# Moving the last z2 tile behind v, splitting k's first shifted copies, z2's bias on GpSimd, and a new order of products and gates

## The chip, the cores and the metric

The kernel runs on one core of a Trainium2 chip. The metric is the device time of one execution in microseconds (us). Of the kernel before, three runs are shown: 201.68, 201.68 and 201.16, median 201.68. The profile is of an execution of its own.

The engines are TensorE (PE, with PEld for its weight loads), VectorE (DVE), ScalarE (ACT), GpSimd (POOL) and SyncE (SP), which here only issues transfers. Each works through its own list of instructions in order; semaphores join them. Transfers issued by SP, ScalarE and GpSimd go through DMA queues.

## The reference

The input x (2048 positions by 512) is normalised over its 512 channels to xn. Two branches are computed from xn, and x is added:

```python
def _A_ref(x, wqkv, wo):            # 32 heads of 16 channels, W = 8 positions, dilation 2
    q, k, v = heads of (x @ wqkv)
    idx = pos[:, None] - 2 * arange(8)[None, :]     # this position and 7 before it
    logits = einsum('bhsd,bhswd->bhsw', q, k[idx]) * 16 ** -0.5   # masked where idx < 0
    o = einsum('bhsw,bhswd->bhsd', softmax(logits), v[idx])
    return o @ wo

def _B_ref(x, w_in, w_sp, b_sp, w_out):             # Fh = 688
    z = gelu(x @ w_in)
    z1, z2 = z[..., :Fh], layernorm(z[..., Fh:])
    g = einsum('ts,bsf->btf', w_sp, z2) + b_sp[None, :, None]
    return (z1 * g) @ w_out

out = x + _A_ref(xn, wqkv, wo) + _B_ref(xn, w_in, w_sp, b_sp, w_out)
```

## The kernel before

The 2048 positions are 16 tiles of 128. All steps are named, each has a list of steps that it needs (`op_(name, needs, f)`), and the order on every engine is written out by hand in five lists at the end (`pe`, `act`, `dve`, `pool`, `sp`). The lists set the order on each engine; waits between engines follow from the data.

TensorE's list is one long row: transposes of xn (T), the z2 half of x @ w_in (z0 to z15, L231), k and q in turns (k0 ... q7, L324), v (v0 to v7, L324), the z1 half (y2 to y15, L231; y0 and y1 earlier), the mixing by w_sp (M0 to M15, L467: each tile M_j sums over all 16 tiles of z2), then the two output products (gf, re: L511 and L516; ao: L523). z, k, q, v, y and M write into three PSUM tiles `mm` in turn, so each waits until the tile of the product three places before it has been read: by `h` (gelu of z), `kc`, `qc`, `vc` (copies of k, q, v), `yg` (gelu of y) or `G` (M plus b_sp), all on ScalarE.

z2 is normalised per position. For tiles 8 to 15 ScalarE takes the sum in the gelu (h, L249) and the sum of squares (sq, L277). Then for four tiles at a time, 8 to 11 and 12 to 15: `zs` on VectorE (L281 to L283) makes mean and variance, `zr` on GpSimd (L287, a scale, and L288, a power) the reciprocal root, `zb` (L292) the bias, and `zn` on ScalarE (L304) scales each tile in place. M0 needs all `zn`.

The attention has four channels of a head at a time (c = 0 to 3) and two halves of the positions (th = 0, 1). k's rows carry 16 positions from the half before them; these shifted copies are `kh` (L342 and L343, two DMAs each). kh0 and kh1 are issued by SP, kh2 and kh3 by GpSimd, and `vh` is the same for v, on SP. For each c and th VectorE forms the products `m` (L358, two instructions of 2.29 us), `f` folds their second half onto the first by an adding DMA issued by GpSimd (L366, two DMAs; f00 alone is an add on VectorE), and `p` (L371, or L373 and L374) sums into the logits. There are four buffers for the products: a product takes a buffer when the `p` of its last user is done. Then follow the softmax (X, e, u, i, C) and the weighted sum of v, twelve VectorE instructions a half (a0.0 to a1.11, L425 to L438), between which stand the gates `g` (L483: z1 times G). Each gated tile is turned by SP (`U`, L473 to L476) and is needed by the output products: the tiles 8 to 15 by gf2.

Of W_sp, 256 rows at a time are loaded and transposed by SP (W0 to W7) into three buffers. The third is also a product buffer, so W2 waits until all `p` are done (HW).

Of the kernel before, what the change touches and what calls it, by code (L numbers as in the profile page):

```python
# [10 lines left out]
ALU = mybir.AluOpType  # L11
# [5 lines left out]
NT = S // P  # L17
# [9 lines left out]
FH = 688  # L27
# [15 lines left out]
def kernel(  # L43
# [13 lines left out]
    V = nc.vector  # L57
    A = nc.scalar
    G = nc.gpsimd
    PE = nc.tensor  # L60
    SP = nc.sync

    x2 = A_x.rearrange("b s d -> (b s) d")
# [13 lines left out]
    zsum = sb.tile([P, NT], F32, name="zsum")  # L77
    zsq = sb.tile([P, NT], F32, name="zsq")
    zmean = sb.tile([P, NT], F32, name="zmean")
    zvar = sb.tile([P, NT], F32, name="zvar")  # L80
    zrstd = sb.tile([P, NT], F32, name="zrstd")
    zbias = sb.tile([P, NT], F32, name="zbias")
    b16 = sb.tile([NT, P], BF16, name="b16")
# [15 lines left out]
    k_c = [r[:, QC:QC + KC].rearrange("p (d t s) -> p d t s", d=DC, t=2) for r in qk_c]  # L99
# [50 lines left out]
    def op_(name, after, f):  # L150
        assert name not in do, name
        do[name], needs[name] = f, list(after)
# [125 lines left out]

    def z2_stats(i, n):
        s = slice(i, i + n)  # L280
        V.tensor_scalar(zmean[:, s], zsum[:, s], 1.0 / FH, None, ALU.mult)  # L281
        V.tensor_tensor(zvar[:, s], zmean[:, s], zmean[:, s], ALU.mult)  # L282
        V.scalar_tensor_tensor(zvar[:, s], zsq[:, s], 1.0 / FH, zvar[:, s], ALU.mult, ALU.subtract)  # L283

# [4 lines left out]

    def z2_bias(i, n):  # L290
        s = slice(i, i + n)
        V.scalar_tensor_tensor(zbias[:, s], zmean[:, s], -1.0, zrstd[:, s], ALU.mult, ALU.mult)  # L292

    for i in range(0, 8, 4):
        op_(f"zr{i}", [f"zt{i + x}" for x in range(4)], lambda i=i: z2_bn_root(i, 4))
    for i in range(8, NT, 4):
        op_(f"zs{i}", [f"sq{i + x}" for x in range(4)], lambda i=i: z2_stats(i, 4))
        op_(f"zr{i}", [f"zs{i}"], lambda i=i: z2_root(i, 4))
        if i in ZACT:
            op_(f"zb{i}", [f"zr{i}"], lambda i=i: z2_bias(i, 4))  # L300
# [39 lines left out]
    def halo(eng, x):  # L340
        y = x.rearrange("p d t s -> p (d t) s")
        eng.dma_start(y[H:P, :, 0:HALO], y[0:P - H, :, GS:GS + HALO])  # L342
        eng.dma_start(x[0:H, :, 1, 0:HALO], x[P - H:P, :, 0, GS:GS + HALO])  # L343

    for c in range(NC):
        op_(f"kh{c}", [f"kc{2 * c}", f"kc{2 * c + 1}"], lambda c=c: halo(SP if c < 2 else G, k_c[c]))
    op_("vh", [f"vc{p}" for p in range(8)], lambda: halo(SP, vp[:]))


    last = {}  # L350

    def products(c, th):
        for a in range(2):
            pr = ph[BUF[c, th]][a].rearrange("p (w b s) -> p w b s", w=W, b=2)
            k = k_c[c][:, 2 * a:2 * a + 2, th, :]
            k = bass.AP(k.tensor, k.offset + HALO - DIL * (W - 1), [k.ap[0], [DIL, W], k.ap[1], [1, GS]])
            q = q_c[c][:, 2 * a:2 * a + 2, th, :].unsqueeze(1).broadcast_to([P, W, 2, GS])
            V.tensor_tensor(pr, q, k, ALU.mult)  # L358

    def fold(c, th):  # L360
        x = PU // 4
        if (c, th) == (0, 0):
            V.tensor_tensor(ph[0][0], ph[0][0], ph[0][1], ALU.add)
            return
        for n in range(2):
            G.dma_start(*[h[:, n * x:(n + 1) * x] for h in ph[BUF[c, th]]], accum_op=ALU.add)  # L366

    def logits(c, th):
        pr = ph[BUF[c, th]][0].rearrange("p (w b s) -> p w b s", w=W, b=2)
        if c == 0:  # L370
            V.tensor_tensor(a_sb[:, th], pr[:, :, 0], pr[:, :, 1], ALU.add)  # L371
        else:
            V.tensor_tensor(pr[:, :, 0], pr[:, :, 0], pr[:, :, 1], ALU.add)  # L373
            V.tensor_tensor(a_sb[:, th], a_sb[:, th], pr[:, :, 0], ALU.add)  # L374

    for c, th in BUF:
        n = f"{c}{th}"
        b = BUF[c, th]
        over = {2: ALLN + ALLX, 3: [f"p{1}{0}"] + [f"{a}{p}" for a in "qk" for p in range(8)]}.get(b, [])
        op_(f"m{n}", over + [f"qc{2 * c}", f"qc{2 * c + 1}", f"kh{c}"] + ([last[b]] if b in last else []),  # L380
            lambda c=c, th=th: products(c, th))
        op_(f"f{n}", [f"m{n}"], lambda c=c, th=th: fold(c, th))
        op_(f"p{n}", [f"f{n}"], lambda c=c, th=th: logits(c, th))
        last[b] = f"p{n}"
# [174 lines left out]
    for n, c in enumerate(halves):  # L559
        i = groups[3][3]  # L560
# [2 lines left out]


    pe = """wu T0a T0 z0a z0A T1 z0B T2 z1 T3 z2 T4 z3 T5 z4 T6 z5 T7 B z6 z7 y0 y1 z8 z9 z10 z11 z12 z13 z14
        k0 k1 q0 q1 z15 k2 k3 q2 q3 k4 k5 q4 q5 k6 k7 q6 q7
        v0 v1 v2 v3 v4 v5 v6 v7 y2 y3 y4 y5 y6 y7 y8 y9 y10 y11 y12 y13 y14 y15
        M0 M1 M2 M3 M4 M5 M6 M7 M8 M9 M10 M11 M12 M13 M14 M15
        gf0 gf1 re0 re1 ao0 ao1 gf2 re2 re3 ao2 ao3""".split() + [f"gf3.{i}" for i in tail[:3]] + ["gfl0", "gfl1"]
    for n in pe:  # L570
        a, x = n[0], n[1:]
# [19 lines left out]
    op_("EL", ["yg15"], lambda: A.preload_act_table_set("natural_log_exp_and_others"))  # L591

    act = """wz0 wz1 GL Tc0a Tc0 Tc1 Tc2 h0 Tc3 h1 Tc4 h2 Tc5 h3 Tc6 h4 Tc7 Bc h5 h6 h7 yg0 yg1 h8 h9 sq8 h10 h11 sq9 h12 h13 h14 sq10
        kc0 sq11 kc1 qc0 sq12 qc1 h15 kc2 sq13 kc3 sq14 qc2 sq15 qc3 kc4 kc5 qc4 qc5 kc6 kc7 qc6 qc7
        vc0 zn8 vc1 zn9 vc2 zn10 vc3 zn11 vc4 zn12 vc5 zn13 vc6 zn14 vc7 zn15
        yg2 yg3 yg4 yg5 yg6 yg7 yg8 yg9 yg10 yg11 yg12 yg13 yg14 yg15 EL
        G0 e0 G1 i0 e1 G2 i1 G3 G4 G5 G6 G7 G8 G9 G10 G11 G12 G13 G14 G15""".split()
    act += [f"E{i}" for n in (0, 1) for i in groups[n]]
    dve = """b0 ag0 b1 ag1 n0a n0 b2 ag2 n1 b3 ag3 n2 b4 ag4 n3 b5 ag5 n4 b6 ag6 b7 n5""".split()
    for i in range(6, NT):  # L600
        dve += [f"ag{i + 1}"] * (i + 1 < NT) + [f"b{i + 2}"] * (i + 2 < NT) + [f"n{i}"]
    dve += """zt0 zt1 zt2 zt3 zt4 zt5 zn0 zn1 zn2 zn3 zt6 zt7 zn4 zn5 zn6 zn7
        m00 f00 p00 m01 zs8 m10 zb8 zs12 m11 p01 zb12 m20 p10 m21 p11 m30 p20 m31 p21 p30 X0 p31 HW u0 X1 C0 g0 a0.0 u1 a0.1 C1 g1 g2
        a0.2 g3 a0.3 g4 a0.4 g5 a0.5 a0.6 g6 a0.7 g7 a0.8 a0.9 g8 a0.10 a0.11 g9 g10 a1.0 a1.1 g11 a1.2 g12 a1.3 g13
        a1.4 g14 a1.5 a1.6 g15 a1.7 a1.8 a1.9 a1.10 a1.11""".split()
    OUT = [i for n in range(3) for i in groups[n]] + tail[:3]
    dve += [f"F{i}" for i in OUT] + ["Fl0", "Fl1"]
    pool = ["b16"] + [f"gr{i}" for i in range(NT)] + "zr0 zr4 f01 zr8 kh2 f10 zr12 kh3 f11 f20 f21 f30 f31".split()
    sp = """x0 x1 x2 x3 x4 x5 x6 x8 wy x12 wk wq wv t8 t9 t10 t11 t12 t13 t14 t15 W0 kh0 W1 kh1 vh
        W2 W3 LO0 LO1 W4 U0 W5 LO2 LO3 U1 U2 W6 LO4 U3 U4 W7 U5 U6 U7 U8 U9 U10 R0 U11 U12 U13 R1 U14 U15""".split()  # L610
    sp += [f"S{i}" for i in OUT] + ["Sl0"]
    act.append("Sl1")
# [52 lines left out]
```

## Time and profile before

| | |
|---|---|
| runs shown, median | 201.68 us (201.16 to 201.68) |
| the profiled execution's own time | 201.17 us |
| its span in the profile | 199.4 us |
| TensorE busy | 194.3 us, 97% |
| VectorE busy | 177.5 us, 89% |
| ScalarE busy | 89.7 us, 45% |
| GpSimd busy | 39.0 us, 20% |
| granted TensorE clock | 1.00 in every stage looked at |

The span is what the engines' records cover; the execution's own time is 1.8 us longer. Times in the rows that follow are from the start of the span. A row of the chain in order of time is: start, length, what. A row of a timeline is: start, length, engine, line, operation, output <- input, shapes, count, and in brackets the idle time of that engine ahead of it with what ended it. Consecutive instructions of one kind are merged into one row; an instruction's record can begin a little ahead of the end of the one before. "SPq" rows are issues of transfers. A row "DMA to landing" gives the shortest, median and longest time from the start of an issue to the arrival of its data.

### The profile page before, as it was taken

Reading aid. Unit: us, or ns where it says so; the run is one execution under the profiler, and the core shown is the slowest. Engines: PE = TensorE matmul, PEld = TensorE weight load, DVE = VectorE, ACT = ScalarE, POOL = GpSimd, SP = SyncE. Lnnn points to the kernel's source line nnn. Section 1 sums busy time; section 2 is a strip of 40 time slices with the busy share of each in tenths; the row PEclk is TensorE's granted clock in tenths of the full one; section 3 lists DMA queues with packets and bytes.
Section 4 is the critical chain, followed back from the end, with each engine's and each line's share of the span. In section 5 each row is a group of like instructions: output and inputs, shape, how many; then the busy total and the mean of one; then the engine's idle time right before and its main releaser. Section 6 shows DMA issues by size and latency. Waiting matters only on the chain.

```text
span 199.4 us, 4530 instructions
## 1 busy us (share of the span) xinstructions
PE 194.3 (97%) x1935; PEld 122.5 (61%) x1935; DVE 177.5 (89%) x204; ACT 89.7 (45%) x130; POOL 39.0 (20%) x67
## 2 busy tenths in 40 slices
PE   7899999999999999999999999999999999999993
PEld 2576666666777766666666666666666654443441
DVE  4999895899898999988999999999999999997234
ACT  2597797795559996672542311112221110043000
POOL 5677122002999330330000000000000000000000
PEclk9999999999999999999999999999999999999999
DMA  5999476840977999998099999999996679914233
GB/s 163 349 361 230 89 123 139 144 81 0 196 132 140 197 196 147 185 167 168 11 234 229 188 168 227 237 123 258 198 230 60 118 219 233 154 19 133 81 105 105
DMA packets 68964, 32.58 MB, mean 163 GB/s; under 512 B 56912, under 2 KB 67024, under 8 KB 68816
## 3 DMA queue, kind: packets, MB, share of 16 engines
q1 hardware_dynamic: 65568, 24.12, 59.5%
q0 software_dynamic: 2176, 7.40, 20.0%
q10 hardware_dynamic: 1200, 0.77, 1.4%
q8 instruction: 15, 0.25, 0.5%
q14 instruction: 5, 0.04, 0.1%
HBM read 10.03 MB, written 2.10 MB: 61 GB/s over the span
## 4 chain that ended last, share of the span: by engine, by line
PE 95%; DMA 3%; DVE 1%; ACTq 0%; DVEq 0%; issue 0%
PE mm L467 37%; PE mm L324 21%; PE mm L231 19%; PE mm L523 7%; PE mm L511 7%; DMA wts<-in_B_w_in_dram 3%; PE aux L511 2%; PE mm L516 1%; PE aux L213 1%; ACTq L239 0%; DVE z L561 0%; DVEq L660 0%; DVE wsp L129 0%; PE aux L523 0%; DVE qk L139 0%
## 5 line engine op out<-in xcount | busy, mean ns | idle before, releaser
L467 PE MATMUL mm<-z,wsp 128*128 128x344 bf16 x512 | 74.8, 309 | 0.0
L467 PEld LDWEIGHTS <-wsp 128*128 128x128 bf16 x512 | 50.1, 98 | 24.6
L324 PE MATMUL mm<-xnT,wts 128*32 128x512 bf16 x768 | 41.9, 380 | 0.0
L231 PE MATMUL mm<-wts,xnT 128*128 128x344 bf16 x256 | 39.0, 309 | 0.5 <-ACT xnT L216 0.5
L324 PEld LDWEIGHTS <-wts 128*32 128x32 bf16 x768 | 29.5, 140 | 12.0 <-issue 0.6
L425 DVE TENSOR_TENSOR prod<-vp,a_sb 128x4096 bf16<-128x4096 bf16 x16 | 36.1, 2285 | 0.0
L481 ACT ACTIVATE qk<-mm,b_col 128x688 bf16<-128x688 f32 x16 | 13.3, 830 | 45.3 <-PE mm L467 38.3
L231 PEld LDWEIGHTS <-xnT 128*128 128x128 bf16 x256 | 24.4, 98 | 13.0 <-issue 1.0
L358 DVE TENSOR_TENSOR prod<-qk 128x4096 bf16<-128x4096 bf16 x12 | 27.0, 2288 | 1.8 <-DMA qk<-qk 1.6
L429 DVE TENSOR_TENSOR prod<-prod,prod 128x8192 bf16<-128x8192 bf16 x6 | 26.5, 4420 | 0.0
L337 ACT CAST qk<-mm 128x1024 bf16<-128x1024 f32 x16 | 16.2, 1012 | 7.8 <-PE mm L324 7.8
L313 ACT ACTIVATE z<-mm 128x688 bf16<-128x688 f32 x16 | 11.8, 748 | 5.7 <-PE mm L231 5.3
L366 POOL DMA_DIRECT2D prod<-prod x10 | 8.7, 1022 | 28.3 <-DVE zvar L282 16.0
L523 PE MATMUL mm<-wts,xnT 32*128 32x512 bf16 x192 | 14.2, 374 | 0.0
L511 PEld LDWEIGHTS <-qk 128*128 128x128 bf16 x85 | 8.2, 98 | 9.4 <-issue 0.8
L511 PE MATMUL mm<-wts,qk 128*128 128x512 bf16 x60 | 13.6, 379 | 0.0
L249 ACT ACTIVATE z<-mm 128x688 bf16<-128x688 f32 x16 | 11.9, 745 | 1.9 <-PE mm L231 1.8
L170 DVE BATCH_NORM_STATS2 stats<-z 128x6 f32<-128x512 bf16 x16 | 10.8, 673 | 1.7 <-DMA z<-in_A_x_dram 1.7
L523 PEld LDWEIGHTS <-xnT 32*128 32x128 bf16 x256 | 6.3, 93 | 7.7 <-issue 0.8
L556 DVE TENSOR_TENSOR z<-mm,wsp 128x512 bf16<-128x512 f32 x6 | 3.8, 684 | 8.0 <-PE mm L523 4.8
L550 ACT CAST z<-mm 128x512 bf16<-128x512 f32 x6 | 3.2, 598 | 13.7 <-PE mm L523 12.3
L177 POOL TENSOR_TENSOR rstd<-rstd,mhalf 128x1 f32<-128x1 f32 x16 | 9.0, 561 | 1.3
(82 smaller groups left out, 169.6 us busy)
## 6 DMA issues: line engine op xcount, KB each, us to landing
prod<-prod POOLq DMA_DIRECT2D x10, 512.0 KB, 7.6
wts<-in_A_wo_dram SPq DMA_DIRECT2D x4, 512.0 KB, 6.3
wsp<-in_A_x_dram SPq DMA_DIRECT2D x2, 1024.0 KB, 6.5
out_dram<-z SPq DMA_DIRECT2D x15, 128.0 KB, 1.8
wts<-in_A_wqkv_dram SPq DMA_DIRECT2D x3, 512.0 KB, 8.6
z<-in_A_x_dram SPq DMA_DIRECT2D x2, 512.0 KB, 6.4
wsp<-z POOLq DMA_DIRECT2D x2, 512.0 KB, 6.5
wsp<-wts POOLq DMA_DIRECT2D x2, 512.0 KB, 8.9
```

Of the source, the lines that this page charges most:

```text
L231: PE.matmul(t[:, hh, 0:FHALF], xnT[:, kc, i * P:(i + 1) * P], w_z[part][:, kc, hh * FHALF:(hh + 1) * FHALF], start=(kc == 0), stop=(kc == ...
L249: A.activation(z2[:, i, :].rearrange("p (a b) -> p a b", a=2), t[:, :, 0:FHALF], ACT.Gelu_apprx_tanh, **total)
L313: op_(f"yg{i}", [f"y{i}"], lambda: A.activation(z1u[:, i, 0:FH].rearrange("p (a b) -> p a b", a=2), t[:, :, 0:FHALF], ACT.Gelu_apprx_tanh))
L324: PE.matmul(t[32 * g:32 * g + 32, dd, :], w, r, start=(kc == 0), stop=(kc == C - 1), tile_position=(0, 32 * g))
L337: op_(f"{a}c{p}", [f"{a}{p}"], lambda: A.copy(home(a, p), t[:].rearrange("p d (t s) -> p d t s", t=2)))
L358: V.tensor_tensor(pr, q, k, ALU.mult)
L425: return lambda: V.tensor_tensor(dst, vp[:, :, th, off:off + GS], a_sb[:, th, W - 1 - w].unsqueeze(1).broadcast_to([P, DH, GS]), ALU.mult)
L429: return lambda: V.tensor_tensor(dst, dst, x, ALU.add)
L467: PE.matmul(t[:, hh, 0:FHALF], w[:, k, (j % 2) * P:(j % 2 + 1) * P], z2[:, k, hh * FHALF:(hh + 1) * FHALF], start=(k == 0), stop=(k == NT ...
L481: lambda: A.activation(gs[j % 3].rearrange("p (a b) -> p a b", a=2), t[:, :, 0:FHALF], ACT.Identity, bias=b_col[:, j:j + 1]))
L511: PE.matmul(po[i][:, c], uT[th][:, m, t0:t0 + P], wout[:, m, c], start=(start and m == 0), stop=(stop and m == MF - 1))
L523: PE.matmul(po[groups[n][g]], op[32 * g:32 * g + 32, th, d, s * P:(s + 1) * P], wo_r[32 * g:32 * g + 32, d, :], start=(start and d == 0), ...
```

## The change

Four things are edited; the arithmetic stays.

- In TensorE's list z15 goes from between q1 and k2 to between v7 and y2. In ScalarE's list h15 and sq15 go behind vc7. zn8 to zn11 start one copy of v later, and zn12 to zn15 stand between yg9 and yg13, each ahead of a gelu of z1.
- kh0 becomes two steps, kh0a behind kc0 and kh0b behind kc1, each with two DMAs for two of the four channels. The first half of m00 depends on the first pair alone.
- zs8 and zs12 write the mean with the other sign, and the bias is a plain product on GpSimd in place of one on VectorE. zb8 stands behind zr8 and ahead of kh2 in GpSimd's list.
- In VectorE's list zs12 goes from behind m10 to behind m30, in GpSimd's list zr12 goes from behind f10 to behind f30 with zb12 after it, ahead of f31. The gates g13, g14 and g15 stand later among the steps of a1.

```diff
-        V.tensor_scalar(zmean[:, s], zsum[:, s], 1.0 / FH, None, ALU.mult)
+        V.tensor_scalar(zmean[:, s], zsum[:, s], -1.0 / FH, None, ALU.mult)
...
-        V.scalar_tensor_tensor(zbias[:, s], zmean[:, s], -1.0, zrstd[:, s], ALU.mult, ALU.mult)
+        G.tensor_tensor(zbias[:, s], zmean[:, s], zrstd[:, s], ALU.mult)
...
-        op_(f"kh{c}", [f"kc{2 * c}", f"kc{2 * c + 1}"], lambda c=c: halo(SP if c < 2 else G, k_c[c]))
+        if c == 0:
+            for a in range(2):
+                op_(f"kh0{'ab'[a]}", [f"kc{a}"], lambda a=a: halo(SP, k_c[0][:, 2 * a:2 * a + 2]))
+        else:
+            op_(f"kh{c}", [f"kc{2 * c}", f"kc{2 * c + 1}"], lambda c=c: halo(SP if c < 2 else G, k_c[c]))
...
# pe
-        k0 k1 q0 q1 z15 k2 k3 q2 q3 k4 k5 q4 q5 k6 k7 q6 q7
-        v0 v1 v2 v3 v4 v5 v6 v7 y2 y3 y4 y5 y6 y7 y8 y9 y10 y11 y12 y13 y14 y15
+        k0 k1 q0 q1 k2 k3 q2 q3 k4 k5 q4 q5 k6 k7 q6 q7
+        v0 v1 v2 v3 v4 v5 v6 v7 z15 y2 y3 y4 y5 y6 y7 y8 y9 y10 y11 y12 y13 y14 y15
# act
-        kc0 sq11 kc1 qc0 sq12 qc1 h15 kc2 sq13 kc3 sq14 qc2 sq15 qc3 kc4 kc5 qc4 qc5 kc6 kc7 qc6 qc7
-        vc0 zn8 vc1 zn9 vc2 zn10 vc3 zn11 vc4 zn12 vc5 zn13 vc6 zn14 vc7 zn15
-        yg2 yg3 yg4 yg5 yg6 yg7 yg8 yg9 yg10 yg11 yg12 yg13 yg14 yg15 EL
+        kc0 sq11 kc1 qc0 sq12 qc1 kc2 sq13 kc3 sq14 qc2 qc3 kc4 kc5 qc4 qc5 kc6 kc7 qc6 qc7
+        vc0 vc1 zn8 vc2 zn9 vc3 zn10 vc4 zn11 vc5 vc6 vc7 h15 sq15
+        yg2 yg3 yg4 yg5 yg6 yg7 yg8 yg9 zn12 yg10 zn13 yg11 zn14 yg12 zn15 yg13 yg14 yg15 EL
# dve
-        m00 f00 p00 m01 zs8 m10 zb8 zs12 m11 p01 zb12 m20 p10 m21 p11 m30 p20 m31 p21 p30 X0 p31 HW u0 X1 C0 g0 a0.0 ...
-        ... a1.3 g13 a1.4 g14 a1.5 a1.6 g15 a1.7 a1.8 a1.9 a1.10 a1.11
+        m00 f00 p00 m01 zs8 m10 m11 p01 m20 p10 m21 p11 m30 zs12 p20 m31 p21 p30 X0 p31 HW u0 X1 C0 g0 a0.0 ...
+        ... a1.3 a1.4 g13 a1.5 g14 a1.6 a1.7 g15 a1.8 a1.9 a1.10 a1.11
# pool
-    zr0 zr4 f01 zr8 kh2 f10 zr12 kh3 f11 f20 f21 f30 f31
+    zr0 zr4 f01 zr8 zb8 kh2 f10 kh3 f11 f20 f21 f30 zr12 zb12 f31
# sp
-    ... t15 W0 kh0 W1 kh1 vh
+    ... t15 W0 kh0a kh0b W1 kh1 vh
```

More of the change, by code (lines that the diff above doesn't have):

```diff
@@ L379 @@
         over = {2: ALLN + ALLX, 3: [f"p{1}{0}"] + [f"{a}{p}" for a in "qk" for p in range(8)]}.get(b, [])
-        op_(f"m{n}", over + [f"qc{2 * c}", f"qc{2 * c + 1}", f"kh{c}"] + ([last[b]] if b in last else []),
+        op_(f"m{n}", over + [f"qc{2 * c}", f"qc{2 * c + 1}"] + (["kh0a", "kh0b"] if c == 0 else [f"kh{c}"]) + ([last[b]] if b in last else []),
             lambda c=c, th=th: products(c, th))
@@ L602 @@
     dve += """zt0 zt1 zt2 zt3 zt4 zt5 zn0 zn1 zn2 zn3 zt6 zt7 zn4 zn5 zn6 zn7
-        m00 f00 p00 m01 zs8 m10 zb8 zs12 m11 p01 zb12 m20 p10 m21 p11 m30 p20 m31 p21 p30 X0 p31 HW u0 X1 C0 g0 a0.0 u1 a0.1 C1 g1 g2
-        a0.2 g3 a0.3 g4 a0.4 g5 a0.5 a0.6 g6 a0.7 g7 a0.8 a0.9 g8 a0.10 a0.11 g9 g10 a1.0 a1.1 g11 a1.2 g12 a1.3 g13
-        a1.4 g14 a1.5 a1.6 g15 a1.7 a1.8 a1.9 a1.10 a1.11""".split()
+        m00 f00 p00 m01 zs8 m10 m11 p01 m20 p10 m21 p11 m30 zs12 p20 m31 p21 p30 X0 p31 HW u0 X1 C0 g0 a0.0 u1 a0.1 C1 g1 g2
+        a0.2 g3 a0.3 g4 a0.4 g5 a0.5 a0.6 g6 a0.7 g7 a0.8 a0.9 g8 a0.10 a0.11 g9 g10 a1.0 a1.1 g11 a1.2 g12 a1.3
+        a1.4 g13 a1.5 g14 a1.6 a1.7 g15 a1.8 a1.9 a1.10 a1.11""".split()
     OUT = [i for n in range(3) for i in groups[n]] + tail[:3]
     dve += [f"F{i}" for i in OUT] + ["Fl0", "Fl1"]
-    pool = ["b16"] + [f"gr{i}" for i in range(NT)] + "zr0 zr4 f01 zr8 kh2 f10 zr12 kh3 f11 f20 f21 f30 f31".split()
-    sp = """x0 x1 x2 x3 x4 x5 x6 x8 wy x12 wk wq wv t8 t9 t10 t11 t12 t13 t14 t15 W0 kh0 W1 kh1 vh
+    pool = ["b16"] + [f"gr{i}" for i in range(NT)] + "zr0 zr4 f01 zr8 zb8 kh2 f10 kh3 f11 f20 f21 f30 zr12 zb12 f31".split()
+    sp = """x0 x1 x2 x3 x4 x5 x6 x8 wy x12 wk wq wv t8 t9 t10 t11 t12 t13 t14 t15 W0 kh0a kh0b W1 kh1 vh
         W2 W3 LO0 LO1 W4 U0 W5 LO2 LO3 U1 U2 W6 LO4 U3 U4 W7 U5 U6 U7 U8 U9 U10 R0 U11 U12 U13 R1 U14 U15""".split()
```

## The prediction

> **What bounds the kernel now.** I read the chain that ended last first, then TensorE's neighbours on each engine around its stages. The page gives the chain by engine, and the chain in order of time gives the stages (start us, length us, what):
>
> ```profile
> PE 95%; DMA 3%; DVE 1%; ACTq 0%; DVEq 0%; issue 0%
> ```
> ```profile
> 28.38 7.07 PE mm L324 x128
> 35.45 1.27 PE mm L231 x8
> 36.72 34.70 PE mm L324 x534
> 71.43 16.44 PE mm L231 x112
> 87.87 74.67 PE mm L467 x512
> ...
> 179.15 4.42 PE mm L511 x20
> ```
>
> TensorE has no gap from the first product to the last: k and q around z15 (28.38 to 71.43, v included), y2 to y15 (71.43 to 87.87, 16.44/14 = 1.174 us each), then M0. The other engines matter only where they make TensorE late. There is nothing to take from TensorE's own work except a change of product form around z15, while every microsecond by which M0 begins after 87.87 is a microsecond on the end. So the question is what releases y13, y14, y15 and M0 afterwards. Each takes the PSUM tile that the gelu three products earlier (yg10 to yg13) empties on ScalarE, and the change puts zn12 to zn15 in ScalarE's order right there.
>
> ScalarE before (the copies and gelus by time; the bracket is the idle time in front):
>
> ```profile
> 30.32 1.01 ACT L337 CAST qk<-mm 128x1024 bf16<-128x1024 f32 x1 [0.31 <-PE mm L324]
> 33.78 1.01 ACT L337 CAST qk<-mm 128x1024 bf16<-128x1024 f32 x1 [0.71 <-PE mm L324]
> ...
> 60.31 0.97 ACT L304 ACTIVATE z<-z,zbias,zrstd 128x688 bf16<-128x688 bf16 x1
> 61.18 1.00 ACT L337 CAST vp<-mm 128x1024 bf16<-128x1024 f32 x1
> ...
> 73.48 1.41 ACT L313 ACTIVATE z<-mm 128x688 bf16<-128x688 f32 x2
> 80.90 0.74 ACT L313 ACTIVATE z<-mm 128x688 bf16<-128x688 f32 x1 [0.42 <-PE mm L231]
> ```
>
> The last row is yg9, done at 81.64. A zn takes 0.87 start to start (60.31 to 61.18), a gelu 0.67 back to back (1.41 - 0.74).
>
> VectorE and GpSimd before:
>
> ```profile
> 35.85 4.50 DVE L358 TENSOR_TENSOR prod<-qk 128x4096 bf16<-128x4096 bf16 x2 [1.65 <-DMA qk<-qk]
> 43.85 4.48 DVE L358 TENSOR_TENSOR prod<-qk 128x4096 bf16<-128x4096 bf16 x2
> 48.26 0.16 DVE L281 TENSOR_SCALAR zmean<-zsum 128x4 f32<-128x4 f32 x1
> 50.97 2.29 DVE L358 TENSOR_TENSOR z<-qk 128x4096 bf16<-128x4096 bf16 x1
> 54.17 0.16 DVE L292 SCALAR_TENSOR_TENSOR zbias<-zmean,zrstd 128x4 f32<-128x4 f32 x1 [0.92 <-POOL zrstd L288]
> 54.73 4.49 DVE L358 TENSOR_TENSOR prod<-qk 128x4096 bf16<-128x4096 bf16 x2
> 59.13 1.22 DVE L371 TENSOR_TENSOR a_sb<-prod 128x2048 bf16<-128x2048 bf16 x1
> 61.28 0.16 DVE L292 SCALAR_TENSOR_TENSOR zbias<-zmean,zrstd 128x4 f32<-128x4 f32 x1 [0.92 <-POOL zrstd L288]
> 65.87 1.22 DVE L373 TENSOR_TENSOR wsp<-wsp 128x2048 bf16<-128x2048 bf16 x1
> 75.36 4.50 DVE L358 TENSOR_TENSOR prod<-qk 128x4096 bf16<-128x4096 bf16 x2
> 79.77 1.22 DVE L373 TENSOR_TENSOR prod<-prod 128x2048 bf16<-128x2048 bf16 x1
> 82.28 4.50 DVE L358 TENSOR_TENSOR prod<-qk 128x4096 bf16<-128x4096 bf16 x2
> ```
> ```profile
> 48.65 1.81 POOL L366 DMA_DIRECT2D prod<-prod  x2 [16.05 <-DVE zvar L282]
> 50.54 0.57 POOL L287 TENSOR_SCALAR zvar<-zvar 128x4 f32<-128x4 f32 x1
> 51.19 2.95 POOL L288 TENSOR_TENSOR zrstd<-zvar,mhalf 128x4 f32<-128x4 f32 x1
> 54.11 0.88 POOL L342 DMA_DIRECT2D qk<-qk  x1
> 55.58 1.85 POOL L366 DMA_DIRECT2D wsp<-z  x2
> 57.50 1.77 POOL L287 TENSOR_SCALAR zvar<-zvar 128x4 f32<-128x4 f32 x1
> 59.35 1.89 POOL L288 TENSOR_TENSOR zrstd<-zvar,mhalf 128x4 f32<-128x4 f32 x1
> 80.15 1.70 POOL L366 DMA_DIRECT2D prod<-prod  x2 [5.28 <-DVE prod L358]
> ```
>
> A tiny GpSimd operation ends when a VectorE product of two inputs does. The scale at 57.50 ends at 59.27, just behind m11 (54.73 + 4.49 = 59.22). The power at 59.35 ends at 61.24, which is 0.89 behind the end of p01's add (60.35); the one at 51.19 ends at 54.14, 0.88 behind m10 (53.26). So each costs the rest of the VectorE instruction that is running, plus 0.05 (scale) or 0.89 (power).
>
> **Part by part.**
>
> *k's first copies in two pieces.* One pair of DMAs becomes two: kh0a behind kc0 (done 31.33), kh0b behind kc1. On the SP queue and to landing:
>
> ```profile
> 33.09 0.76 SPq L342 DMA_DIRECT2D qk<-qk  x1
> 33.90 0.64 SPq L343 DMA_DIRECT2D qk<-qk  x1
> ```
> ```profile
> DMA to landing us min/median/max: 1.8/1.8/1.8
> ```
>
> kh0a's two issues (0.76 + 0.64) end by 32.8, ahead of kh0b's place at 33.09, so W1, kh1 and vh behind them on SP are not moved. Its second copy is issued at about 32.2 and lands at 34.0. m00's first half then waits only for qc0 (33.78 + 1.01 = 34.79); kh0b lands near 35.7, and the second half starts at 37.1. VectorE is 1.0 us earlier: m00 34.85, m01 ends 47.35. Were the issue not hidden, its 1.4 us would fall on VectorE, which has cover.
>
> *z15 behind v.* k2 to v7 move 1.27 us forward and z15 takes 70.16 to 71.43; y2 stays. The switch to z15 and back disappears: 7.07 us for 32 groups of four is 0.221 a group, 34.70 for 160 is 0.217, so about 0.1 us is gained (bounds 0 and 0.2). h15 and sq15 follow vc7 and end near 73.3, so yg2 stays near 73.4: nothing. But zs12 now can't be earlier than 73.3.
>
> *Bias on GpSimd.* Two VectorE instructions of 0.16 go, and their waits of 0.92 each. zs12 leaves its place behind m10 too. By the rows, m11 starts 54.73 - 53.26 = 1.47 sooner behind m10, and m20, which now directly follows p01, some 1.1 sooner. A tiny TENSOR_TENSOR on GpSimd, zb8, is added: its nearest row is the scale, the rest of a VectorE instruction plus 0.05. It stands ahead of kh2 and f10 in GpSimd's queue. With everything 0.97 earlier: f01 47.68 to 49.49, scale to 50.13, power to 53.17, then zb8 waits for m11's first half (52.2 + 2.29) and ends at 54.55. kh2's two issues take 55.58 - 54.11 = 1.47 and f10 is issued at 56.1, against 55.58 before. f10's landing, before (two halves):
>
> ```profile
> DMA to landing us min/median/max: 4.7/6.5/8.4
> ```
>
> The second half starts 0.95 into the 1.85 and lands 8.4 later: 64.9 before, 65.45 now. kh2 must have landed when m20 starts; for m20 (4.49) to hide in front of 65.45 it has until 60.9, five microseconds after issue. So p10 begins at 65.45, against 65.87: **VectorE's gain goes into a new wait for f10.** p10, m21, p11, m30 last from 65.87 to 79.86 = 13.99, so m30 ends at T = 79.44.
>
> *zs12 behind m30, zr12 and zb12 behind f30.* zs12: three instructions, 0.5 us (48.26 to m10 at 48.76 before). Then VectorE has p20's two adds (to T + 2.9; 79.77 to 82.28 is 2.51) and m31's halves (to T + 5.2 and T + 7.4). GpSimd: f30 starts T + 0.29 (80.15 - 79.86) and takes 1.70, T + 2.0. The scale waits for p20: T + 2.96. The power starts in m31's first half, T + 5.2, + 0.89 = T + 6.1. zb12 waits for m31's second half: T + 7.5. That is **87.0**. Bounds: 5.3 where one boundary is caught instead of missed, 8.5 where the power holds VectorE up (below). I take 7.5, by the rows of zr8 and zr12, which each missed theirs. f31 is queued behind zb12 on GpSimd and needs m31, which ends at T + 7.4 itself: it goes out 0.1 us later than it could, and with it p31, the release of W2's buffer and W2, which M4 needs some 19 us behind M0's start: nothing.
>
> *zn12 to zn15 among the gelus.* ScalarE stands behind yg9 (81.64) until 87.05. Then zn12, yg10, zn13, yg11, zn14, yg12, zn15, yg13: 4 x 0.87 + 3 x 0.67 + 0.74 = 6.2 us, as y10 to y12 are long done. yg10 is done at 88.7, so y13, due at 84.35, begins 4.4 late; y14 and y15 wait for yg11 and yg12 (about 0.4 each), M0 for yg13: 93.3. **M0 is 5.4 us late**, and nothing behind it can give that back.
>
> *Gates g13 to g15 later.* g15 comes behind one more sum:
>
> ```profile
> 164.47 0.51 DVE L483 TENSOR_TENSOR z<-qk,z 128x688 bf16<-128x688 bf16 x1
> 164.90 4.42 DVE L429 TENSOR_TENSOR prod<-prod,prod 128x8192 bf16<-128x8192 bf16 x1
> ...
> 170.81 1.23 SPq L476 DMA_TRANSPOSE qk<-z  x1
> ```
>
> By about 4.6 us, to 169.6; its transposes would be issued 1 us later than before, to 173, and are needed at 179.15 (later still with M late). Cost nothing; without that cover it is at most that 1 us.
>
> Sum: 201.17 (the profiled execution; span 199.4) + 5.4 - 0.1 = **206.5**. The median of the runs shown, 201.68, stands 0.5 above the profiled one.
>
> The Trainium skill, SBUF — State Buffer, section "Who interferes with whom", says that a VectorE instruction with two SBUF inputs and a GpSimd instruction that reads SBUF exclude each other, whichever came first holding the port pair for its whole length. The waits above agree (57.50 to 59.27); in both power rows VectorE was waiting anyway, so no row shows the other direction.
>
> **The rivals.**
>
> *The power holds VectorE back.* If VectorE can't run during the granted 0.89 us, m11 starts at 53.2, zb8 ends at 55.5, f10 goes out at 57.05 and lands at 66.4: T = 80.4, m31's second half ends at T + 8.4, zb12 at 88.9, M0 at 95.1: +7.2, 208.3. For it: the exclusion seen one way. Against: the power's reading may be short. That page of the Trainium skill, with its lock for the whole length, would give this result.
>
> *Boundaries caught, f10 early.* With zb8 through right behind the power (53.4), f10 is issued at 54.9, lands 64.2, T = 78.2; with T + 5.3, zb12 at 83.5 and M0 at 89.8: 203.0. For anything between, time follows zb12 one to one.
>
> *The split brings nothing* (kh0a held up in the queue): m00 at 35.85, all GpSimd steps 0.97 later, f10 lands 66.4, zb12 88.0: 207.4.
>
> *Not slower: zb12 is ready by 81.64.* Then ScalarE never stands still: zn and gelus from 81.64 put yg13 at 87.9, M0 0 to 0.2 late, less 0.1: 201.2. It needs T at 76.3 or less with the short chain of 5.3, that is f10 landed by 62.3; without any wait of VectorE T would be 79.86 - 1.0 - 1.5 - 1.1 = 76.3. f10 before landed 9.35 after its issue, so it would have to be issued by 53.0, before the power is done. Against.
>
> **How the numbers follow.** 0.3%, 0.6 us, is about what a measurement of this kernel can tell from no change. Forecast 206.5 (205.3 to 207.2) 0.46; power holding 208.3, 0.18; split without effect 207.4, 0.10; early boundaries 203.0 to 205.3, 0.17; not slower 201.2, 0.07; unforeseen 0.02. The range 203.0 to 208.8 leaves out the last two and the tails. Faster by over 0.3% 0.02, within 0.06, slower 0.92.
>
> **What would show it.** The longest wait of ScalarE is L304 for GpSimd's bias, about 5 us, after the tenth gelu of z1; TensorE idles at L231 for gelus, 5 us in all, and M0 starts near 93.3. The wait of m00 for DMA is gone; one for f10's DMA at p10 of 2 to 3 us appears. The power at zr12 takes over 2 us. Wrong would be: M0 near 88, or GpSimd's tiny operations passing in between products.

## The result and the profile after

The changed kernel takes 208.02 us (median of 6 runs, 207.12 to 210.17) against 201.56 us: 1.0338 times the time before, 95% interval 1.0298 to 1.0377. The profiled execution took 207.59 us, its span is 205.8 us. That is 6.4 us more than the profiled execution before. Ratios compare undisturbed executions; a single one, of 727 us in the run with zs12 early, is left out of them.

The chain by engine, from the page, and the chain in order of time around the place (start us, length us, what):

```profile
PE 68%; DVE 12%; issue 9%; POOL 5%; DMA 2%; ACT 1%; SPq 1%; DVEq 0%; ACTq 0%; POOLq 0%
```
```profile
82.49 3.08 POOL zrstd L288
...
85.66 1.29 POOL zbias L292
...
87.84 0.73 ACT z L313
...
88.62 5.34 PE mm L231 x24
93.95 74.67 PE mm L471 x512
```

Before, the chain stayed on TensorE from its first product of k to M0 and on. Now it leaves TensorE, runs over GpSimd's power and bias (zr12, zb12) and one gelu (yg10), and comes back for y13 to y15 (24 products). M0 starts at 93.95 instead of 87.87. The mixing then takes 74.67 us in both; the end comes 0.3 us later behind M0 than before, which is taken up below. The waits of the profile after (engine, line, what was waited for: us in total, times, longest):

```profile
ACT z L304 <- POOL zbias L292: 5.1, 1, 5.1
...
PE mm L231 <- ACT z L313: 4.0, 1, 4.0
...
DVE wsp L377 <- DMA wsp<-z: 2.5, 1, 2.5
```

These are ScalarE in front of zn12, TensorE in front of y13, and VectorE at p10 for f10's data. On the three engines the way there looks like this:

```profile
35.35 4.50 DVE L362 TENSOR_TENSOR prod<-qk 128x4096 bf16<-128x4096 bf16 x2 [0.60 <-ACT qk L337]
...
50.47 2.28 DVE L362 TENSOR_TENSOR z<-qk 128x4096 bf16<-128x4096 bf16 x1
52.67 4.49 DVE L362 TENSOR_TENSOR prod<-qk 128x4096 bf16<-128x4096 bf16 x2
...
65.39 1.23 DVE L377 TENSOR_TENSOR wsp<-wsp 128x2048 bf16<-128x2048 bf16 x1 [2.52 <-DMA wsp<-z]
...
74.89 4.50 DVE L362 TENSOR_TENSOR prod<-qk 128x4096 bf16<-128x4096 bf16 x2
...
81.13 1.22 DVE L378 TENSOR_TENSOR a_sb<-a_sb,prod 128x2048 bf16<-128x2048 bf16 x1
82.39 4.49 DVE L362 TENSOR_TENSOR prod<-qk 128x4096 bf16<-128x4096 bf16 x2
```
```profile
50.69 2.95 POOL L288 TENSOR_TENSOR zrstd<-zvar,mhalf 128x4 f32<-128x4 f32 x1
53.72 1.30 POOL L292 TENSOR_TENSOR zbias<-zmean,zrstd 128x4 f32<-128x4 f32 x1
...
56.44 1.87 POOL L370 DMA_DIRECT2D wsp<-z  x2
...
79.68 1.72 POOL L370 DMA_DIRECT2D prod<-prod  x2 [5.26 <-DVE zvar L282]
81.48 0.93 POOL L287 TENSOR_SCALAR zvar<-zvar 128x4 f32<-128x4 f32 x1
82.49 3.08 POOL L288 TENSOR_TENSOR zrstd<-zvar,mhalf 128x4 f32<-128x4 f32 x1
85.66 1.28 POOL L292 TENSOR_TENSOR zbias<-zmean,zrstd 128x4 f32<-128x4 f32 x1
```
```profile
81.16 0.74 ACT L313 ACTIVATE z<-mm 128x688 bf16<-128x688 f32 x1 [0.42 <-PE mm L231]
86.98 0.96 ACT L304 ACTIVATE z<-z,zbias,zrstd 128x688 bf16<-128x688 bf16 x1 [5.08 <-POOL zbias L292]
87.84 0.72 ACT L313 ACTIVATE z<-mm 128x688 bf16<-128x688 f32 x1
```

The product m30 (74.89) ends at 79.39 and the fold f30 is issued. The scale ends at 82.41, just behind p20's second add; the power ends 0.89 behind the first half of m31, the bias just behind its second half (86.94). ScalarE has stood at zn12 since 81.90 and yg10 comes at 87.84.

TensorE, by the timeline and by stages (the stage and its length in us, then busy us of PE, PEld, DVE, ACT, POOL with instruction counts, the granted TensorE clock, DMA share, GB/s):

```profile
81.83 2.79 PE L231 MATMUL mm<-wts,xnT 128*128 128x344 bf16 x18
88.62 5.34 PE L231 MATMUL mm<-wts,xnT 128*128 128x344 bf16 x24 [4.00 <-ACT z L313]
```
```profile
88.62:89.50 0.88, 0.88 (x6) 0.55 (x6) 0.66 (x1) 0.88 (x2) 0.36 (x1) 0.83 1.11 214
89.50:92.50 3.00, 3.00 (x12) 1.64 (x11) 2.63 (x3) 3.00 (x5) 0.00 (x0) 0.50 1.04 197
92.50:93.95 1.45, 1.45 (x12) 0.90 (x10) 1.35 (x4) 1.14 (x2) 0.00 (x0) 0.96 0.96 184
93.95:98.00 4.05, 4.05 (x30) 2.73 (x28) 3.69 (x5) 2.03 (x2) 0.00 (x0) 1.00 0.02 4
```

After 4.0 us without work the granted clock fell: 0.83 on average over the first 0.88 us, 0.50 over the next 3 us, and 1.00 again by the time M0 began. The three products took 5.34 us; at the speed of before they would have taken 3 x 1.174 = 3.5.

### The profile page after: what moved, and what is told of

It reads as the page before. It is cut to its first block, busy times and chain, and to the rows that moved or that the text cites. A ratio compares the mean times of both kernels' runs of the same rounds, so it can differ in the third digit from the quotient of the medians.

```text
span 205.8 us, 4539 instructions
## 1 busy us (share of the span) xinstructions
PE 195.4 (95%) x1935; PEld 122.0 (59%) x1935; DVE 177.9 (86%) x202; ACT 89.7 (44%) x130; POOL 42.1 (20%) x69
## 4 chain that ended last, share of the span: by engine, by line
PE 68%; DVE 12%; issue 9%; POOL 5%; DMA 2%; ACT 1%; SPq 1%; DVEq 0%; ACTq 0%; POOLq 0%
PE mm L471 36%; PE mm L231 12%; DVE prod L362 8%; PE mm L527 7%; PE mm L515 6%; PE mm L324 3%; DMA z<-in_A_x_dram 2%; PE aux L515 2%; POOL prod L370 2%; POOL zrstd L288 1%; DVE a_sb L375 1%; DVE prod L367 1%; DVE z L362 1%; PE mm L520 1%; POOL wsp L370 1%
## 5 line engine op out<-in xcount | busy, mean ns | idle before, releaser
L231 PE MATMUL mm<-wts,xnT 128*128 128x344 bf16 x256 | 40.7, 318 | 4.8 <-ACT z L313 4.0
L324 PEld LDWEIGHTS <-wts 128*32 128x32 bf16 x768 | 28.5, 138 | 13.0 <-issue 0.3
L231 PEld LDWEIGHTS <-xnT 128*128 128x128 bf16 x256 | 25.2, 100 | 18.1 <-issue 5.0
L370 POOL DMA_DIRECT2D prod<-prod x10 | 9.6, 1186 | 22.1 <-DVE zvar L282 20.3
L304 ACT ACTIVATE z<-z,zbias,zrstd 128x688 bf16<-128x688 bf16 x8 | 7.7, 962 | 5.1 <-POOL zbias L292 5.1
L337 ACT CAST vp<-mm 128x1024 bf16<-128x1024 f32 x8 | 8.1, 1010 | 2.7 <-PE mm L324 2.7
```

Source lines behind the costliest of these rows:

```text
L231: PE.matmul(t[:, hh, 0:FHALF], xnT[:, kc, i * P:(i + 1) * P], w_z[part][:, kc, hh * FHALF:(hh + 1) * FHALF], start=(kc == 0), stop=(kc == ...
L324: PE.matmul(t[32 * g:32 * g + 32, dd, :], w, r, start=(kc == 0), stop=(kc == C - 1), tile_position=(0, 32 * g))
L337: op_(f"{a}c{p}", [f"{a}{p}"], lambda: A.copy(home(a, p), t[:].rearrange("p d (t s) -> p d t s", t=2)))
```

## Experiments

Each was timed beside the kernel before on the same chip. They are in the order of what they decide.

**Is it the place of zn12 to zn15 on ScalarE, or the late bias itself?** The first attempt moved them behind yg13, and nothing else:

```diff
- ... yg9 zn12 yg10 zn13 yg11 zn14 yg12 zn15 yg13 yg14 yg15
+ ... yg9 yg10 yg11 yg12 yg13 zn12 zn13 zn14 zn15 yg14 yg15
```

> The changed kernel with zn12 to zn15 moved on ScalarE from between the gelus yg9 to yg13 to behind yg13; the bias zb12 is as late as before (near 87). My theory, that the loss is ScalarE standing still in front of zn12 with the gelus queued behind it: TensorE no longer waits, M0 starts near 88.2 and reads tile 12 of z2 some 3.5 us later, when zn12 is done: 201.4 us (201.0 to 202.0). Rival, that M0 itself can't begin before the last tile is scaled: zn15 ends near 90.8, M0 at 91: about 204.5. Rival, that the loss lies elsewhere (startup, tail, gates): it stays near 207.6.

It took 235.17 us (ratio 1.168, 1.161 to 1.176), and it decides nothing. The second half of m10's products lies in the rows of z1 that yg10 to yg15 write. With zn12 ahead of yg10 the written order had m10 and f10 first; without it, these gelus came first and m10 waited for them (and then overwrote six tiles of z1, so this program no longer computes the same output):

```profile
DVE z L362 <- ACT z L313: 35.8, 1, 35.8
```

A version that joined this order of the gelus with an earlier zs12, zr12 and zb12 (its zb8 stands where the change puts it, whatever the label says) had the same fault:

> The version put together: the changed kernel with zs12 behind p11, zr12 and zb12 ahead of f30, and zn12 to zn15 behind yg13. By my theory neither the bias nor the order on ScalarE can make TensorE wait: 201.3 us (200.9 to 201.8), level with the kernel before or up to 0.2 us under it for z15 no longer standing between k and q. Rival: f30, now 1.4 us later, delays the logits and with them the end: over 202.

234.33 us. The first was run again with yg10 made to follow p10 in the written order; the second, with zb8 behind f10 as well, is the last run below:

```diff
+    needs["yg10"].append("p10")
```

> The changed kernel with zn12 to zn15 behind yg13 on ScalarE, as tried before, and the written order now keeps the gelus yg10 to yg15 behind the fold f10, whose buffer lies in their rows. The bias is as late as in the changed kernel (near 87). My theory, that the loss is the gelus queued behind zn12: no wait of TensorE, M0 near 88, its products with tiles 12 to 15 of z2 come 3.5 us later and find them scaled: 201.5 us (201.0 to 202.2). Rival, that M0 needs all tiles at its first product: M0 near 91, 204.5. Rival, another cause: near 207.6.

201.70 us, ratio 1.0005 (0.9977 to 1.0034). The bias came as late as in the changed kernel, 86.87, and TensorE did not wait. GpSimd, ScalarE and TensorE of this run:

```profile
85.59 1.28 POOL L292 TENSOR_TENSOR zbias<-zmean,zrstd 128x4 f32<-128x4 f32 x1
```
```profile
85.83 0.74 ACT L313 ACTIVATE z<-mm 128x688 bf16<-128x688 f32 x1 [0.42 <-PE mm L231]
86.91 3.52 ACT L304 ACTIVATE z<-z,zbias,zrstd 128x688 bf16<-128x688 bf16 x4 [0.34 <-POOL zbias L292]
```
```profile
70.45 17.67 PE L231 MATMUL mm<-wts,xnT 128*128 128x344 bf16 x120
87.96 10.22 PE L471 MATMUL mm<-z,wsp 128*128 128x344 bf16 x69
```

z15 to y15 are one row without a gap, and M0 begins near 88 (87.96 by this row, whose records begin a little early; 88.12 by the chain). The first of tiles 12 to 15 of z2 is scaled by then and the last by 90.43; M0 comes to tile 12 after 24 products, some 3.5 us after its start. So the loss is the gelus queued behind zn12, and a bias at 87 is early enough for M0 itself.

**Is the late bias the other half of it?** zs12 behind p11, zr12 and zb12 ahead of f30; ScalarE's order as in the changed kernel:

```diff
- ... m21 p11 m30 zs12 p20 ...        - ... f20 f21 f30 zr12 zb12 f31
+ ... m21 p11 zs12 m30 p20 ...        + ... f20 f21 zr12 zb12 f30 f31
```

> The changed kernel with zs12 behind p11 instead of m30 on VectorE, and zr12 and zb12 ahead of f30 on GpSimd; ScalarE's order is that of the changed kernel. If the lateness of the bias alone makes the loss: zs12 ends near 75.3, the scale waits for m30's first half (77.6), the power for its second (79.8 + 0.9), the bias for p20's first add: zb12 near 81, before yg9 is done (81.9). M0 near 88.2, 201.4 us (201.0 to 202.2). If GpSimd's small operations are held longer than one VectorE instruction each, zb12 is at 83 to 85 and the time 203 to 205. If interleaving itself (zn and gelu by turns) is too slow for TensorE, M0 is some 0.5 to 1 us late with no idle ScalarE.

201.61 us, ratio 0.9996 (0.9964 to 1.0028). The bias was ready before yg9 was done, and zn and gelu by turns (0.86 + 0.62 start to start) did not make TensorE wait:

```profile
80.75 0.22 POOL L292 TENSOR_TENSOR zbias<-zmean,zrstd 128x4 f32<-128x4 f32 x1
```
```profile
80.89 0.74 ACT L313 ACTIVATE z<-mm 128x688 bf16<-128x688 f32 x1 [0.42 <-PE mm L231]
81.53 0.95 ACT L304 ACTIVATE z<-z,zbias,zrstd 128x688 bf16<-128x688 bf16 x1
82.39 0.73 ACT L313 ACTIVATE z<-mm 128x688 bf16<-128x688 f32 x1
```

Either repair alone suffices: the loss needs both the late bias and gelus behind it.

**Does the time follow the bias one to one?** zr12 and zb12 behind f31:

```diff
- ... f30 zr12 zb12 f31
+ ... f30 f31 zr12 zb12
```

> The changed kernel with zr12 and zb12 behind f31 instead of ahead of it: only the bias is later. f31 goes out 87.2 to 88.9; the scale ends at p21's end (89.3), the power has VectorE's wait for f30's data and ends near 90.4, the bias waits for p30's first add: zb12 near 91.1 (90.5 to 93), 4.2 later than in the changed kernel. If the time follows the bias one to one: 211.8 us (211.2 to 213.5). If the loss had another cause, or something else bounds the end by then: under 210.

211.53 us, ratio 1.0471 (1.0416 to 1.0526). The bias came at 90.26, 3.3 later than in the changed kernel (91.1 was expected), the median is 3.5 longer. This execution began its products of k 0.2 earlier (28.70 against 28.91), so measured from there the bias is 3.5 later too. Beside VectorE's wait for data the bias takes 0.19, against 1.28 beside its products:

```profile
90.07 0.19 POOL L292 TENSOR_TENSOR zbias<-zmean,zrstd 128x4 f32<-128x4 f32 x1
```

**Does f10's data set m30, and with it the bias?** zb8 behind kh2 and f10:

```diff
- ... zr8 zb8 kh2 f10 kh3 ...
+ ... zr8 kh2 f10 zb8 kh3 ...
```

> The changed kernel with zb8 behind kh2 and f10 instead of ahead of them on GpSimd; zn8 is due at 61, zb8 is then done near 57.2 at m11's end. Theory, that the way from f10's data by p10, m21, p11 and m30 sets the bias zb12: f10 goes out 1.3 sooner (55.2), p10 starts near 64.1 instead of 65.4, zb12 near 85.6 instead of 86.9, and M0 is 1.3 sooner: about 206.3 us in the profiled execution against 207.59, the median near 206.7. Rival, that VectorE's own work sets m30: no change, 207.6 to 208. Rival, that f11 (behind zb8 now) takes f10's place as the late one: 0.5 gained at most.

205.93 us, ratio 1.0221 (1.0176 to 1.0267); profiled 205.98 against 207.59, 1.6 less. f10 went out at 54.81 instead of 56.44, p10 started at 63.77 instead of 65.39, and the bias ended at 85.32 instead of 86.94: 1.6 at every step. Of this, 0.27 is only the earlier start of this execution (first product of k at 28.64 instead of 28.91); 1.35 is left for the place of zb8, where 1.3 was expected. f10's data took as long as in the changed kernel, 8.96 us from the first issue to p10 against 8.95.

```profile
63.77 1.23 DVE L377 TENSOR_TENSOR wsp<-wsp 128x2048 bf16<-128x2048 bf16 x1 [1.16 <-DMA wsp<-z]
```
```profile
84.04 1.28 POOL L292 TENSOR_TENSOR zbias<-zmean,zrstd 128x4 f32<-128x4 f32 x1
```

**What is the slow clock worth?** 19 products into an unused PSUM tile in the gap ahead of y13:

```diff
+    op_("fill", ["y12", "Bc"], lambda: [PE.matmul(aux[1][:], xnT[:, 0, 0:P], xnT[:, 0, 0:D], start=True, stop=True) for _ in range(19)])
- ... y12 y13 y14 y15
+ ... y12 fill y13 y14 y15
```

> The changed kernel with 19 products of 128x512 into an unused PSUM tile between y12 and y13 on TensorE (their result is not used), some 4.1 us of work in the place of the idle time. Theory, that the three products y13 to y15 took 5.34 us instead of 3.50 because the granted clock was 0.58 behind the idle time: with the gap filled the clock stays at 1.00, y13 to y15 go at full speed but wait for yg11 and yg12, and M0 for yg13: M0 near 93.1 instead of 93.95, 206.8 us in the profiled execution. Rival, that the clock falls for another reason: clock and time as in the changed kernel, 207.6 or a little more.

206.65 us, ratio 1.0241 (1.0194 to 1.0288); profiled 206.81, 0.8 less than the changed kernel with 4 us more work on TensorE.

```profile
84.22 4.26 PE L461 MATMUL aux<-xnT 128*128 128x512 bf16 x19
88.55 1.33 PE L231 MATMUL mm<-wts,xnT 128*128 128x344 bf16 x8
90.03 1.33 PE L231 MATMUL mm<-wts,xnT 128*128 128x344 bf16 x8 [0.15 <-ACT z L313]
91.51 1.33 PE L231 MATMUL mm<-wts,xnT 128*128 128x344 bf16 x8 [0.15 <-ACT z L313]
92.99 5.26 PE L473 MATMUL mm<-z,wsp 128*128 128x344 bf16 x35 [0.15 <-ACT z L313]
```

The granted clock is 1.00 in all of this stretch. Each product now goes at full speed and then waits for its gelu; from y13 to M0 it is 4.4 us instead of 5.3. The clock was low because TensorE had been idle, and that cost 0.9 us beyond the waits which it covered.

**The parts alone, on the kernel before.** k's copies in two pieces:

> The kernel before with only k's first shifted copies in two pieces. m00 starts near 34.9 instead of 35.85 and VectorE is 1 us ahead until m20, which waits for GpSimd as before or a little less; TensorE does not wait for any of it: 201.2 to 201.7 us, no change. Rival, that VectorE's earlier end lets the tail go sooner: at most 0.3 us faster.

201.61 us, ratio 1.0017 (0.9989 to 1.0045): no change that the runs can tell. The traces show a small one at the very end. From SP's last issue of output to the end of the span it is 2.9 us in the kernel before (196.49 to 199.4) and 3.3 here (196.73 to 200.0):

```profile
196.49 0.33 SPq L562 DMA_DIRECT2D out_dram<-z  x1
```
```profile
196.73 0.33 SPq L566 DMA_DIRECT2D out_dram<-z  x1
```

It is 2.9 in all four traces with k's first copies in one piece (before, the gates, the two runs of the bias) and 3.2 to 3.3 in all ten with two pieces, the changed kernel among them (202.57 to 205.8). So some 0.3 us goes with the split; by what way is not shown. The gates:

> The kernel before with only the gates g13 to g15 later among the sums of the second half. g15 near 169.6 instead of 164.5, its transposes issued until near 173, landed near 177, needed at 179.15: no change, 201.2 to 201.7. Rival: the transposes are late and gf2 waits, up to 1 us.

201.25 us, ratio 0.9997 (0.9970 to 1.0025): no change. The bias on GpSimd, with zb8 and zb12 each directly behind its power:

> The kernel before with only the bias on GpSimd (zb8 behind zr8, zb12 behind zr12, both ahead of the shifted copies and folds that follow). Each bias waits for the VectorE product that runs (1 to 2.2 us instead of 0.16), f10 goes out near 57 instead of 55.6, p10 waits for its data until near 66.4 instead of starting at 65.9; zb8 and zb12 are still done before zn8 and zn12 are due. VectorE about 0.5 us behind, TensorE untouched: 201.2 to 201.8 us, no change. Rival: a late bias or a late fold reaches TensorE: over 202.2.

202.79 us, ratio 1.0085 (1.0053 to 1.0117): here I was wrong, and the rival of a late fold (over 202.2) came true. TensorE waited 2.0 us in front of M4, and the memset that releases W2's buffer was 4.2 later than before. TensorE, then VectorE's memset in this run and in the kernel before, and W2's landing in this run:

```profile
108.86 26.41 PE L467 MATMUL mm<-z,wsp 128*128 128x344 bf16 x180 [1.99 <-DVE z L483]
```
```profile
102.17 0.06 DVE L448 MEMSET wsp<- 1x1 uint32 x1
```
```profile
97.95 0.06 DVE L448 MEMSET wsp<- 1x1 uint32 x1
```
```profile
DMA to landing us min/median/max: 6.5/6.5/6.5
```

The profile names a gate (L483) that ended at the same moment, but M4 does not need it. In the code M4 needs the scaled tiles, W2 and the PSUM tile that G1 reads, and G1 was done at 102.40. W2, issued at 102.26, lands 6.5 later, at 108.8; M4 begins at 108.86. The two biases put 1.8 and up to 0.2 us, and the scale and power behind them more, ahead of kh2, f10, kh3 and f11, and each fold was late in turn. The same part with zb8 behind f10 and zb12 behind f11:

```diff
- ... zr8 zb8 kh2 f10 zr12 zb12 kh3 f11 f20 ...
+ ... zr8 kh2 f10 zb8 zr12 kh3 f11 zb12 f20 ...
```

> The kernel before with only the bias on GpSimd, as in the run of the bias alone, but zb8 behind f10 and zb12 behind f11 instead of ahead of the shifted copies. Theory for the 1.7 us that the bias alone cost: the two waits ahead of kh2, f10, kh3 and f11 delay the folds, with them the logits, the release of W2's buffer (102.2 instead of 98) and W2 itself, which M4 then waits for (2 us). Now f10 goes out near 55.9 and f11 near 64.4 (66.9 there, 62.7 before): the buffer is released by 99.5, W2 lands before M4 is due at 106.5, TensorE does not wait: 201.3 us (201.0 to 201.8). Rival, that GpSimd's work itself or another wait made the loss: near 202.8.

201.39 us, ratio 0.9995 (0.9981 to 1.0009). The buffer was released at 99.92, and TensorE has no gap there:

```profile
99.92 0.06 DVE L448 MEMSET wsp<- 1x1 uint32 x1
```

So the cost was the place in GpSimd's queue, not the operation. That W2's landing held M4 up is read from the times and the code; no run moves W2 alone.

**All repairs together:** zn12 to zn15 behind yg13, zs12 behind p11, zr12 and zb12 ahead of f30, zb8 behind f10.

> The changed kernel with zn12 to zn15 behind yg13 (the order of the gelus and f10 kept), zs12 behind p11, zr12 and zb12 ahead of f30, zb8 behind f10. No wait of TensorE is left that the change brought; z15 behind v is worth 0.1 to 0.3 us: 201.2 us (200.8 to 201.7), level with the kernel before within what can be measured. Rival: it beats the kernel before by more than 0.3%, which would need TensorE's own work to be shorter; rival: W2 comes late because f30 goes out later, over 202.

201.84 us, ratio 0.9996 (0.9971 to 1.0021). No version found beats the kernel before: the 0.28 us that z15 behind v gives (below) is about what the end loses with the split copies.

## Why the prediction was right, point by point

Forecast 206.5, measured 208.02, inside the range of 203.0 to 208.8. The mechanism is the one described, but the size was under-estimated: 5.3 us more were forecast and 6.4 came. The chosen case's own band, 205.3 to 207.2, holds neither the median nor the profiled 207.59, and by the number alone the rivals at 207.4 and 208.3 would fit as well; it is the trace that tells them apart.

- *k's copies.* m00's wait for DMA is gone and it starts 6.44 us behind the first product of k (35.35 - 28.91) instead of 7.47: 1.03, as said (1.0). None of this second reached the end, where the split even goes with 0.3 us more (above).
- *The gain goes into f10.* f10 56.44, p10 65.39 with a wait of 2.52; forecast 56.1, 65.45 and 2 to 3 us. The run with zb8 behind f10 shows that this link is real. That p10 came out to 0.06 us is luck: f10 went out 0.34 later than forecast (the execution began 0.53 later), and its data came 0.4 sooner behind it. The forecast put f10's second DMA 0.95 behind the first; in both kernels it starts 0.6 behind (55.6 and 56.2 before, 56.4 and 57.0 after), and it landed 8.3 later instead of 8.4.
- *zs12, zr12, zb12.* T = 79.39 and the bias at 86.94; forecast 79.44 and 87.0, by the same luck: measured from the first product of k, both are 0.6 earlier than forecast. The steps from p10 on are as forecast: the scale, power and bias ended at the VectorE instructions named.
- *The power holds VectorE back: refuted.* m11 started at 52.67, right behind m10, though the power ran until 53.64; m31's two halves took their usual 4.49 around the second power. GpSimd waits for VectorE here, not the reverse. Of the rule in the Trainium skill, SBUF — State Buffer, section "Who interferes with whom", the trace bears out the one direction; that GpSimd's operation, once it has the ports, stops VectorE for its whole length is not what these rows show.
- *ScalarE and the gelus.* zn12 stood 5.1 us, yg10 ended at 88.56 (forecast 88.7), TensorE waited 4.0 (4.4; y12 itself ended 0.27 later here, since the start was 0.53 later and z15's move gave 0.26 back). The sign "5 us in all" did not come: the rest of the loss is not idle time but slow products.
- *z15 behind v* was mis-sized: forecast 0.1, bounds 0 and 0.2. From the first product of k to M0 it is 59.21 us in the run with zs12 early (28.65 to 87.86) and 59.49 before: 0.28.
- *The term that was missing: the clock.* Behind y13 I counted three waits of about 0.35 (y14, y15 and M0), 1.05 together, with the products at full speed. In their place the three products took 5.34 instead of 3.50: 1.84, and the waits vanished in it. The difference is 0.8; filling the gap gave back 0.9 in this stage and 0.8 in the profiled time.
- *The rest.* The profiled execution started its first products 0.53 later (the loading of x and of the weights, not touched by the change) and ended 0.32 later behind M0, which is the end seen in every trace with the split copies. Sum: 0.53 - 0.26 + 4.00 + 1.84 + 0.32 = 6.43, against 6.42 measured. The start varies in the other runs too: k's first product came at 28.64 with only k's copies split and at 29.75 with only the gates moved. Neither start nor end was part of the forecast.
- *Gates at no cost:* confirmed alone. *Bias on GpSimd at no cost beside f10's delay:* true in the changed kernel. The way by f31 and W2 was called "nothing", and the memset that releases W2's buffer came at 97.65, against 97.95 before; with M0 on time again (zs12 early, memset at 97.38) M4 does not wait either. Alone, with zr12 and zb12 ahead of kh3 and f11, the same bias brings W2 too late. The change has them behind f30.

## What to carry to other kernels

On an engine that works in order, ask of every instruction with a late input what stands behind it: four small scalings cost some 6 us here because the gelus that free PSUM stood behind the first of them, and nothing when the same scalings, just as late, stood behind those gelus. When small operations move to GpSimd, count for each the rest of the VectorE instruction that is running, and look at which transfers GpSimd issues after them. When TensorE is to stand idle for more than 2 us, add what a lower clock behind the gap can cost (0.9 us here, beyond the waits).

## What the runs showed of the hardware that was not expected

The prediction has no term for the granted clock, and the clock fell behind shorter gaps than the one forecast (4.4 us). By stages, first behind a gap of 2.65 us (the run with zb8 behind f10), then behind one of 2.0 us (the bias alone):

```profile
86.99:90.50 3.51, 3.51 (x14) 1.96 (x14) 1.47 (x2) 3.51 (x5) 0.36 (x1) 0.55 1.04 195
```
```profile
108.86:112.40 3.54, 3.54 (x25) 2.38 (x26) 3.51 (x3) 1.01 (x2) 0.00 (x0) 1.00 1.22 240
```

After 2.65 us the next 3.5 us ran at 0.55 (24 products took 5.34 us, as after 4.0 us); after 2.0 us the clock stayed at 1.00. These are single profiled executions. All four executions of the run with zb8 behind f10 have a mean clock of 0.989 or 0.990; of the ten of the bias alone nine have 0.997 or more, and the tenth, 204.53 us, has 0.990, so it may have lost the clock after about 2 us as well. Of the six executions of the changed kernel, three have 0.990 or 0.991 (207.12 to 207.92 us) and three 0.981 to 0.984 (208.13 to 210.17 us): the longer ones also had the lower clock. None of these three was profiled, so what made them longer stays open.

The fall did not come at the restart but a little after it: the first 0.51 us behind the gap of 2.65 ran at 0.87 and the next 3 us at 0.50, much as behind the gap of 4.0 us above. Behind 7.5 us (the bias later) the clock had fallen within the gap, and the 24 products took 5.76 us.

The Trainium skill, TensorE: Matmul & The Clock Gate, section "Why this matters for your kernels", sets the limit at gaps of about 3 us; the gap of 2.65 us lies below it and the clock fell. In the return to full speed after some 4 us of work the trace agrees with that page: behind the gap of 4.0 us the products began again at 88.62, and the clock was 0.96 on average from 92.50 to 93.95 and 1.00 behind that.
